# All k and q of slots 6 to 23 transposed by DMA, with token tiles of 4,2,2,2,2,4,4,4 slots

## The chip, the cores and the metric

The kernel runs on one core of a Trainium2 chip. The metric is device time in microseconds (us), from the start of one execution to its end. The core has five engines that run side by side, each with its own queue in order: TensorE (PE in the profile; PEld is its weight loads), VectorE (DVE), ScalarE (ACT), GpSimd (POOL) and SyncE (SP), which here only issues DMAs. Matrix products land in PSUM banks, from which ACT or DVE must carry them to on-chip memory (evict them). Sixteen DMA engines move data between on-chip memory and HBM, and can transpose on the way.

## The reference

Two stages. The first is a recurrent linear attention (retention) over 4 sequences of 768 tokens with 8 heads of 64. The second is a bilinear feed-forward layer over the 3072 tokens that result.

```python
gamma = 1.0 - 2.0 ** (-5.0 - np.arange(H))          # one decay for each head
scale = 1.0 / np.sqrt(D)
for t in range(S):
    state = gamma[None, :, None, None] * state + np.einsum('bhd,bhe->bhde', k[:, :, t], v[:, :, t])
    y[:, :, t] = scale * np.einsum('bhd,bhde->bhe', q[:, :, t], state)
x = y.transpose(0, 2, 1, 3).reshape(B * S, H * D)    # 3072 x 512
a = x @ w_a                                          # 512 -> 1536
b = x @ w_b
return (a * b) @ w_out                               # 1536 -> 512
```

Inputs and output are float32; the kernel multiplies in bfloat16 and accumulates in float32.

## The kernel before

**Slots.** The 3072 tokens are cut into 24 slots of 128 tokens, six for each sequence. Slots 0 to 5 are done in pairs by functions of their own (names that end in 2). For slots 6 to 23, `load_slot` (line 84) fetches k, q and v of a slot, 256 KB each, through SP. `casts` (line 221) scales k and q by tables of powers of gamma, which turns the decay into a plain causal product, and converts them and v to bfloat16, all on POOL.

**Transposes.** The attention needs k and q with the head dimension on the partitions (`kqT`). For slots from `ON_PE` = 10 on, `casts` issues one DMA transpose on SP (line 228), and behind it the loads of the slot two further on. For slots 6 to 9, `flip` (line 234) does it on PE with eight transposes into a PSUM bank, and DVE copies the bank out. The loads of slots 6 to 11 stand in the list `LOADS` at the start.

**Turns.** Slots go through the attention two at a time. `turn(new, old)` (line 316) begins two slots and ends the two before. For the new ones it adds k and v products into the state (`update`, whose result is cast to `gst` by the engine given, ACT unless DVE is named), and multiplies k by q (`scores`: the second slot into two banks of the pool `ff`, the first into one of its own; DVE masks both into `aT`). For the old ones it adds the part from the state (`inter`) and the part within the slot (`intra`) into `y`, which ACT copies to `xt` (`leave`). The state is begun anew with each sequence: slots 6, 12 and 18 have no `inter`, and slots 11, 17 and 23 no `update`.

**Token tiles.** The feed-forward layer works on tiles of several slots, listed in `TILES`: 4, 2, 4, 4, 4, 4, 2. For each of twelve blocks of 128 hidden columns, `ffn_ab` makes `a` (four matmuls, evicted by ACT to `asb`) and `g` (four matmuls, multiplied with `asb` by DVE into `ht`). A tile of 4 slots has 512 columns for each matmul, one of 2 slots 256. `ffn_out` makes one slot's output from `ht` with twelve matmuls; ACT evicts it to `osb`. For tiles 0 and 1 the store is held back and issued by SP at the next piece of feed-forward work; from tile 2 on ACT issues it at once (lines 483 to 486). `a`, `g`, output products, flips and the second slot's scores share the three banks of `ff`.

**What sets the order.** Every instruction is chained to the one before it on its engine (`seq`), so each engine works in the order of the program text. From tile 1 on, `run` (line 488) goes through a tile's blocks and outputs and puts turns and flips in at the places given (lines 575 to 586); it calls `casts` for a slot four pieces of work ahead of its flip. The transposed tiles have six buffers, the scaled ones six, the raw loads three pairs, `osb` four. A buffer is written again only once its last reader is done.

Of the kernel before, what the change touches and what calls it, by code (L numbers as in the profile page):

```python
# [10 lines left out]
BF16 = mybir.dt.bfloat16  # L11
# [1 line left out]
ALU = mybir.AluOpType  # L13


TILES = [4, 2, 4, 4, 4, 4, 2]
PAIRS = 3
ON_PE = 10


LOADS = "p0 p1 w0 w1 w2 w3 w4 p2 w5 o0 o1 o2 o3 o4 o5 s6 s7 s8 s9 s10 s11".split()


@with_exitstack
def kernel(
# [10 lines left out]
    nc = tc.nc  # L36
    P = 128
    B, H, S, D = q.shape
    NCH = S // P
    HP = H // 2  # L40
# [3 lines left out]
    NFT = DFF // P  # L44
    NSLOT = B * NCH
# [14 lines left out]
    tra = ctx.enter_context(tc.tile_pool(name="tra", bufs=4))  # L60
# [4 lines left out]
    psff = ctx.enter_context(tc.tile_pool(name="psff", bufs=3, space=bass.MemoryType.PSUM))  # L65
# [7 lines left out]
    def seq(bi):  # L73
        ins = bi.ins
        prev = last.get(ins.engine)
        if prev is not None:
            tc.add_manual_dep(ins, prev.name, nosync, reason="program order")
        last[ins.engine] = ins
        return bi
# [4 lines left out]
    def load_slot(t):  # L84
        b, ci = divmod(t, NCH)
        for nm, src in (("k", k), ("q", q), ("v", v)):
            if t % 2 == 0:
                whole[nm] = raw.tile([P, 2, H, D], F32, tag=nm + "f", name=nm + "f")
            raws[nm, t] = whole[nm][:, t % 2]
            s = src[b, :, ci * P : (ci + 1) * P, :].rearrange("h p d -> p h d")  # L90
            seq(nc.sync.dma_start(out=raws[nm, t], in_=s))
# [21 lines left out]

    pending = list(LOADS)

# [6 lines left out]
    kqb = {}  # L122
    kqb = {}
# [8 lines left out]
    ident = const.tile([P, P], BF16, name="ident")  # L132
# [45 lines left out]
    def cast(engine, dst, src):  # L178
        if engine is nc.scalar:
            seq(nc.scalar.copy(dst, src))  # L180
        else:
            seq(engine.tensor_copy(dst, src))  # L182
# [10 lines left out]
    kb, qb, vb, kqT, aT = {}, {}, {}, {}, {}  # L193
    state = {}
    xt, where = {}, {}
    first = 0
    for J, n in enumerate(TILES):
        for i in range(n):
# [17 lines left out]
    def new_nat(t):  # L216
        kqb[t] = nat.tile([P, 2, HP, 2, D], BF16, tag="kqb", name="kqb")
        kb[t], qb[t] = kqb[t][:, 0], kqb[t][:, 1]
        vb[t] = nat.tile([P, H, D], BF16, tag="vb", name="vb")

    def casts(t):
        new_nat(t)
        scaled(nc.gpsimd, t, 0)
        scaled(nc.gpsimd, t, 1)
        cast(nc.gpsimd, vb[t], raws["v", t])
        if t >= ON_PE:
            kqT[t] = tra.tile([P, 2, HP, P], BF16, tag="kqT", name="kqT", bufs=6)
            seq(nc.sync.dma_start_transpose(
                out=kqT[t].rearrange("p a b c -> p (a b) c"),
                in_=kqb[t].rearrange("p a hp r d -> p (a hp r d)")))  # L230
            if t + 2 < NSLOT:
                load_slot(t + 2)

    def flip(t):
        if t >= ON_PE:
            return
        tp = psff.tile([P, 2, HP, P], BF16, tag="ff", name="tp")
        for hp in range(HP):
            seq(nc.tensor.transpose(tp[:, 0, hp, :], kb[t][:, hp, :, :], ident))  # L239
        for hp in range(HP):  # L240
            seq(nc.tensor.transpose(tp[:, 1, hp, :], qb[t][:, hp, :, :], ident))  # L241
        kqT[t] = tra.tile([P, 2, HP, P], BF16, tag="kqT", name="kqT", bufs=6)
        seq(nc.vector.tensor_copy(kqT[t], tp))

    def half(i):
        return slice(64 * i, 64 * i + 64)
# [17 lines left out]
    def update(t, eng):  # L264
        ci = t % NCH
        if ci == NCH - 1:
            return
        if ci == 0:
            state[0] = psst.tile([P, HP, D], F32, tag="st", name="st")
        st = state[0]  # L270
        for hp in range(HP):
            for r in range(2):
                seq(nc.tensor.matmul(st[half(r), hp, :], kb[t][:, hp, r, :],  # L273
                                     vb[t][:, HP * r + hp, :],
                                     start=(ci == 0 and hp == 0), stop=(hp == HP - 1),
                                     skip_group_check=True))
        cast(eng, gst[(t + 1) % 4], st)
# [38 lines left out]
    def turn(new, old, eng=nc.scalar):  # L316
        if old is not None:
            ys[old // 2] = [psat.tile([P, 4, P], F32, tag=f"y{r}", name="y") for r in range(2)]
        if new is not None:
            update(new, eng)  # L320
            scores(new + 1, True)
            scores(new, False)
        if old is not None:
            inter(old)
            inter(old + 1)
        if new is not None:
            update(new + 1, nc.scalar)
        if old is not None:
            intra(old)
            intra(old + 1)  # L330
            leave(old)
# [102 lines left out]
    def ffn_a(J, ft, c0=0, c1=None):  # L434
        c1 = TILES[J] * P if c1 is None else c1
        if J not in ht:
# [9 lines left out]
    def ffn_g(J, ft, c0=0, c1=None):  # L446
        c1 = TILES[J] * P if c1 is None else c1
        fs = slice(ft * P, (ft + 1) * P)
        g = psff.tile([P, 4 * P], F32, tag="ff", name="g")[:, : c1 - c0]
        for kt in range(KT):  # L450
            seq(nc.tensor.matmul(g, wb_bf[:, kt, fs], xcols(J, kt, c0, c1),  # L451
                                 start=(kt == 0), stop=(kt == KT - 1)))
        seq(nc.vector.tensor_tensor(ht[J][:, ft, c0:c1], g, asbs.pop((J, ft, c0)), op=ALU.mult))  # L453

    def ffn_ab(J, ft):
        store()
        ffn_a(J, ft)
        ffn_g(J, ft)
# [8 lines left out]
    def ffn_out(J, i):  # L467
        store()
        n0 = (sum(TILES[:J]) + i) * P
        osb = osbp.tile([P, DM], F32, tag="osb", name="osb")  # L470
        ends = J == len(TILES) - 1 and i == TILES[J] - 1
        cols = [(0, DM // 2), (DM // 2, 3 * DM // 4), (3 * DM // 4, DM)] if ends else [(0, DM)]
        for c0, c1 in cols:
            o = psff.tile([P, DM], F32, tag="ff", name="o")[:, : c1 - c0]
            for ft in range(NFT):
                seq(nc.tensor.matmul(o, ht[J][:, ft, i * P : (i + 1) * P], wo_bf[:, ft, c0:c1],  # L476
                                     start=(ft == 0), stop=(ft == NFT - 1)))
            cast(nc.vector if c0 == DM // 2 else nc.scalar, osb[:, c0:c1], o)
            if c0 == DM // 2:
                continue  # L480
            b0 = DM // 2 if c0 else 0
            dst, src = out[n0 : n0 + P, b0:c1], osb[:, b0:c1]
            if J < 2:
                held.append((dst, src))
            else:
                seq((nc.sync if c0 else nc.scalar).dma_start(out=dst, in_=src))

    def run(work, todo, ahead=4):
        order = []
        for g, w in enumerate(work):  # L490
            order += [what for at, *what in todo if at == g]
            order.append(w)
        starts = [a[0] for fn, *a in order if fn is flip]
        for i, (fn, *args) in enumerate(order):
            for fn2, *a2 in order[i : i + ahead + 1]:
                if fn2 is flip and a2[0] in starts:
                    starts.remove(a2[0])
                    casts(a2[0])
            fn(*args)

    D_, G_, A_ = nc.vector, nc.gpsimd, nc.scalar
    K, Q = 0, 1
    warm(11, psat, "y1")
# [64 lines left out]
    ffn_g(0, 11)  # L568
    for j in range(NO):
        cast_o(j)  # L570
    work = [(ffn_ab, 1, ft) for ft in range(NFT)]
    work += [(ffn_out, 0, i) for i in range(TILES[0])]
    work += [(ffn_out, 1, i) for i in range(TILES[1])]
    V_ = nc.vector
    run(work, [(11, flip, 6), (13, flip, 7), (14, turn, 6, None, V_), (14, flip, 8), (15, flip, 9),
               (16, flip, 10), (16, turn, 8, 6, V_), (17, turn, None, 8), (17, flip, 11)])
    todo = {2: [(4, turn, 10, None), (4, flip, 12), (6, flip, 13), (9, turn, 12, 10), (9, flip, 14),
                (10, flip, 15), (13, flip, 16), (14, flip, 17), (14, turn, 14, 12, V_)],
            3: [(4, turn, 16, 14), (4, flip, 18), (6, flip, 19), (9, turn, 18, 16),
                (10, flip, 20), (12, flip, 21)],  # L580
            4: [(4, turn, 20, 18), (4, flip, 22), (6, flip, 23), (9, turn, 22, 20)],
            5: [(4, turn, None, 22)],
            6: []}
    for J in range(2, len(TILES)):
        run([(ffn_ab, J, ft) for ft in range(NFT)] + [(ffn_out, J, i) for i in range(TILES[J])],
            todo[J])


# [28 lines left out]
```

## Time and profile before

| | us |
|---|---|
| median of three runs | 234.96 (233.38 to 236.01) |
| profiled execution | 235.0 |
| its span, first to last instruction | 233.3 |
| PE busy | 224.9 (96%) |
| DVE busy | 95.7 (41%) |
| ACT busy | 83.8 (36%) |
| POOL busy | 78.0 (33%) |
| mean granted TensorE clock | 0.993 |

A row of the page's second part cuts the span into 40 slices of 5.83 us and gives the busy share of each in tenths. The chain that ended last follows the work back from the last instruction, at each step to what released it. A line of a timeline gives the start, the length, the engine, the line of the code, the operation with its tiles, and the count; in brackets stands the idle time before it and what ended that. Matmuls are pipelined, so their recorded lengths overlap; the time from start to start tells what one holds PE for. SPq and ACTq are the DMA issues of SP and ACT.

### The profile page before, as it was taken

The numbers are of one execution on the slowest core, as the hardware profiler recorded it, in microseconds if no ns is written. First come the engines' busy times: TensorE is split into PE (matmuls) and PEld (weight loads), VectorE is DVE, ScalarE is ACT, GpSimd is POOL, SyncE is SP. The second block draws the span as 40 slices with busy tenths as digits, with TensorE's granted clock in tenths as the row PEclk, the third lists the DMA queues.
The fourth block names the chain that finished last, engine by engine and source line by source line (L and its number), as shares of the span: only waits on it lengthen the run. The fifth ranks groups of instructions, "written<-read, shape, count | busy, mean of one in ns | idle before, by whom it ended". The sixth has DMA issues, their size and how long they took to land.

```text
span 233.3 us, 5013 instructions
## 1 busy us (share of the span) xinstructions
PE 224.9 (96%) x2047; PEld 122.4 (52%) x2068; DVE 95.7 (41%) x171; ACT 83.8 (36%) x163; POOL 78.0 (33%) x98
## 2 busy tenths in 40 slices
PE   7879999999999999999999999999999999999995
PEld 2556545587555444545454544454544444445874
DVE  3783338744444264624164630164720233310530
ACT  3362434342215333524344522353422343322422
POOL 4355667787674416454444440000000000000000
PEclk9997999999999999999999999999999999999999
DMA  6999999999999999999999983200002200012102
GB/s 174 290 332 349 343 270 362 368 219 220 198 234 252 273 201 214 173 236 234 250 225 168 240 131 104 90 4 0 3 0 93 90 0 0 0 48 90 45 3 90
DMA packets 91894, 38.59 MB, mean 165 GB/s; under 512 B 71776, under 2 KB 87392, under 8 KB 91872
## 3 DMA queue, kind: packets, MB, share of 16 engines
q1 hardware_dynamic: 89280, 33.69, 64.5%
q10 hardware_dynamic: 2592, 4.59, 5.7%
q8 instruction: 16, 0.26, 0.5%
q14 instruction: 6, 0.05, 0.1%
HBM read 28.31 MB, written 6.29 MB: 148 GB/s over the span
## 4 chain that ended last, share of the span: by engine, by line
PE 80%; DMA 11%; SPq 5%; POOL 1%; issue 1%; ACT 1%; ACTq 0%
PE o L476 27%; PE a L441 23%; PE g L451 23%; DMA wstb<-in_moe_w_b_dram 11%; SPq L97 3%; PE at L257 2%; PE y L302 2%; SPq L105 2%; PE st L273 2%; POOL wb_bf L182 1%; PE y L293 1%; PE tp L239 0%; PE y L406 0%; PE tp L241 0%; ACT osb L180 0%
## 5 line engine op out<-in xcount | busy, mean ns | idle before, releaser
L453 DVE TENSOR_TENSOR ht<-g,asb 128x512 bf16<-128x512 f32 (+1 forms) x86 | 52.0, 604 | 108.0 <-PE g L451 83.1
L441 PE MATMUL a<-xt,wa_bf 128*128 128x512 bf16 (+1 forms) x337 | 76.3, 346 | 1.5 <-POOL wa_bf L182 1.0
L451 PE MATMUL g<-xt,wb_bf 128*128 128x512 bf16 (+1 forms) x341 | 76.3, 347 | 0.4 <-ACT asb L444 0.2
L444 ACT CAST asb<-a 128x512 bf16<-128x512 f32 (+1 forms) x86 | 44.3, 517 | 69.8 <-PE a L441 66.9
L476 PE MATMUL o<-wo_bf,ht 128*128 128x512 bf16 (+2 forms) x303 | 63.7, 362 | 0.5
L451 PEld LDWEIGHTS <-wb_bf 128*128 128x128 bf16 x344 | 33.9, 99 | 29.1 <-issue 0.6
L441 PEld LDWEIGHTS <-wa_bf 128*128 128x128 bf16 x344 | 32.9, 98 | 28.7 <-POOL wa_bf L182 1.2
L476 PEld LDWEIGHTS <-ht 128*128 128x128 bf16 x312 | 29.2, 98 | 31.4
L214 POOL TENSOR_TENSOR kqb<-kf,ktab 128x512 bf16<-128x512 f32 x22 | 22.9, 1043 | 37.0 <-DMA kf<-in_k_dram 36.6
L180 ACT COPY osb<-o 128x512 f32<-128x512 f32 (+2 forms) x25 | 14.1, 565 | 53.5 <-PE o L476 38.0
L262 DVE TENSOR_TENSOR aT<-at,mask 128x512 bf16<-128x512 f32 x36 | 22.3, 680 | 0.0
L182 POOL CAST vb<-vf 128x512 bf16<-128x512 f32 x24 | 15.4, 648 | 12.6 <-DMA vf<-in_v_dram 12.3
L214 POOL TENSOR_TENSOR kqb<-qf,qtab 128x512 bf16<-128x512 f32 x18 | 18.8, 1042 | 1.3 <-DMA qf<-in_q_dram 0.8
L311 ACT CAST xt<-y 128x512 bf16<-128x512 f32 x18 | 9.7, 589 | 3.0 <-PE y L302 3.0
L427 PE MATMUL idle<-zero 128*128 128x512 bf16 x22 | 7.6, 473 | 1.3 <-DVE zero L126 1.3
L370 DVE TENSOR_TENSOR aT<-at,mask 128x512 bf16<-128x512 f32 x12 | 7.4, 681 | 1.1 <-PE at L364 1.1
L182 POOL CAST wb_bf<-wstb 128x1024 bf16<-128x1024 f32 x6 | 6.3, 1042 | 4.1 <-DMA wstb<-in_moe_w_b_dram 4.1
L182 POOL CAST wa_bf<-wsta 128x1024 bf16<-128x1024 f32 x6 | 6.3, 1042 | 2.3 <-DMA wsta<-in_moe_w_a_dram 2.2
L182 POOL CAST wo_bf<-wsto 128x1024 bf16<-128x1024 f32 x6 | 6.3, 1042 | 2.1 <-DMA wsto<-in_moe_w_out_dram 2.1
L180 ACT CAST gst<-st 128x256 bf16<-128x256 f32 x12 | 4.5, 372 | 6.7 <-PE st L273 6.7
L257 PE MATMUL at<-kqT 64*64 64x128 bf16 x288 | 5.8, 219 | 0.0
L302 PE MATMUL y<-aT,vb 128*64 128x128 bf16 x144 | 5.6, 221 | 0.0
(50 smaller groups left out, 83.6 us busy)
## 6 DMA issues: line engine op xcount, KB each, us to landing
kf<-in_k_dram SPq DMA_DIRECT2D x18, 256.0 KB, 4.7
qf<-in_q_dram SPq DMA_DIRECT2D x18, 256.0 KB, 4.9
vf<-in_v_dram SPq DMA_DIRECT2D x18, 256.0 KB, 5.1
out_dram<-osb ACTq DMA_DIRECT2D x17, 256.0 KB, 2.0
wsta<-in_moe_w_a_dram SPq DMA_DIRECT2D x6, 512.0 KB, 8.8
wstb<-in_moe_w_b_dram SPq DMA_DIRECT2D x6, 512.0 KB, 8.9
wsto<-in_moe_w_out_dram SPq DMA_DIRECT2D x6, 512.0 KB, 8.8
kf<-in_k_dram SPq DMA_DIRECT2D x3, 512.0 KB, 7.1
```

Source lines behind the costliest of these rows:

```text
L180: seq(nc.scalar.copy(dst, src))
L182: seq(engine.tensor_copy(dst, src))
L214: seq(eng.tensor_tensor(dst, src, tab, op=ALU.mult))
L257: seq(nc.tensor.matmul(at[r][half(c), hp, :], kqT[t][half(r), 0, hp, half(c)], kqT[t][half(r), 1, hp, :], start=True, stop=True, skip_grou ...
L262: seq(nc.vector.tensor_tensor(aT[t][:, r], at[r], mask.to_broadcast([P, HP, P]), op=ALU.mult))
L302: seq(nc.tensor.matmul(ys[t // 2][r][half(c), 2 * (t % 2) + j, :], vb[t][:, HP * r + hp, :], aT[t][:, r, hp, :], start=begin(t, c, r), sto ...
L311: seq(nc.scalar.copy(xt[J][:, 2 * r : 2 * r + 2, i * P : (i + 2) * P].rearrange("p j (s n) -> p j s n", s=2), ys[t // 2][r].rearrange("p ( ...
L441: seq(nc.tensor.matmul(a, wa_bf[:, kt, fs], xcols(J, kt, c0, c1), start=(kt == 0), stop=(kt == KT - 1)))
L444: seq(nc.scalar.copy(asb, a))
L451: seq(nc.tensor.matmul(g, wb_bf[:, kt, fs], xcols(J, kt, c0, c1), start=(kt == 0), stop=(kt == KT - 1)))
L453: seq(nc.vector.tensor_tensor(ht[J][:, ft, c0:c1], g, asbs.pop((J, ft, c0)), op=ALU.mult))
L476: seq(nc.tensor.matmul(o, ht[J][:, ft, i * P : (i + 1) * P], wo_bf[:, ft, c0:c1], start=(ft == 0), stop=(ft == NFT - 1)))
```

## The change

The PE path for transposes goes, and slots 6 to 9 are transposed by DMA like the others. The loads of slots 8 to 11 leave the list at the start; each is now issued by `casts` behind a transpose. The tiles become 4, 2, 2, 2, 2, 4, 4, 4. In `turn`, where the second new slot has no update (it is a sequence's last), the update of the first moves behind `inter`. The order from tile 1 on, which `run` made, is written out: turns are followed by one, two or three output products of an earlier tile, or by blocks.

```diff
-TILES = [4, 2, 4, 4, 4, 4, 2]
+TILES = [4, 2, 2, 2, 2, 4, 4, 4]
 PAIRS = 3
-ON_PE = 10
-LOADS = "p0 p1 w0 w1 w2 w3 w4 p2 w5 o0 o1 o2 o3 o4 o5 s6 s7 s8 s9 s10 s11".split()
+LOADS = "p0 p1 w0 w1 w2 w3 w4 p2 w5 o0 o1 o2 o3 o4 o5 s6 s7".split()
...
         cast(nc.gpsimd, vb[t], raws["v", t])
-        if t >= ON_PE:
-            kqT[t] = tra.tile([P, 2, HP, P], BF16, tag="kqT", name="kqT", bufs=6)
-            seq(nc.sync.dma_start_transpose(
...
-            if t + 2 < NSLOT:
-                load_slot(t + 2)
-
-    def flip(t):
...
+        seq(nc.sync.dma_start_transpose(
+            out=kqT[t].rearrange("p a b c -> p (a b) c"),
+            in_=kqb[t].rearrange("p a hp r d -> p (a hp r d)")))
+        if t + 2 < NSLOT:
+            load_slot(t + 2)
...
     def turn(new, old, eng=nc.scalar):
...
+        two = new is not None and (new + 1) % NCH < NCH - 1
         if new is not None:
-            update(new, eng)
+            if two or old is None:
+                update(new, eng)
             scores(new + 1, True)
             scores(new, False)
...
-        if new is not None:
+        if two:
             update(new + 1, nc.scalar)
+        elif new is not None and old is not None:
+            update(new, eng)
...
+    casts(6)
+    blocks(1, 0, 3)
+    casts(7)
+    blocks(1, 3, NFT)
+    casts(8)
+    outs(0, 0, 1)
+    casts(9)
+    turn(6, None, V_)
+    outs(0, 2, 3)
+    casts(10)
+    turn(None, 6)
+    outs(1, 0)
+    casts(11)
+    blocks(2, 0, 6)
+    casts(12)
+    turn(8, None, V_)
+    outs(1, 1)
+    casts(13)
+    blocks(2, 6, NFT)
+    turn(10, 8)
+    casts(14)
+    outs(2, 0)
+    blocks(3, 0, 6)
+    casts(15)
+    outs(2, 1)
+    blocks(3, 6, NFT)
+    turn(12, 10, V_)
+    casts(16)
+    outs(3, 0)
+    blocks(4, 0, 3)
+    casts(17)
+    blocks(4, 3, 6)
+    turn(14, 12, V_)
+    casts(18)
+    outs(3, 1)
+    blocks(4, 6, NFT)
+    casts(19)
+    turn(16, 14, V_)
+    casts(20)
+    outs(4, 0, 1)
+    blocks(5, 0, 3)
+    casts(21)
+    blocks(5, 3, 6)
+    turn(18, 16)
+    casts(22)
+    blocks(5, 6, 8)
+    casts(23)
+    blocks(5, 8, NFT)
+    outs(5, 0)
+    turn(20, 18)
+    outs(5, 1, 2, 3)
+    blocks(6, 0, 4)
+    turn(22, 20)
+    blocks(6, 4, 9)
+    turn(None, 22)
+    blocks(6, 9, NFT)
+    outs(6, 0, 1, 2, 3)
+    blocks(7, 0, NFT)
+    outs(7, 0, 1, 2, 3)
```

`blocks(J, a, b)` calls `ffn_ab` for blocks a to b - 1 of tile J, and `outs(J, ...)` calls `ffn_out` for the slots named.

More of the change, by code (lines that the diff above doesn't have):

```diff
@@ L225, in casts @@
         cast(nc.gpsimd, vb[t], raws["v", t])
-        if t >= ON_PE:
-            kqT[t] = tra.tile([P, 2, HP, P], BF16, tag="kqT", name="kqT", bufs=6)
-            seq(nc.sync.dma_start_transpose(
-                out=kqT[t].rearrange("p a b c -> p (a b) c"),
-                in_=kqb[t].rearrange("p a hp r d -> p (a hp r d)")))
-            if t + 2 < NSLOT:
-                load_slot(t + 2)
-    def flip(t):
[L235 to L241, printed above, removed]
-        kqT[t] = tra.tile([P, 2, HP, P], BF16, tag="kqT", name="kqT", bufs=6)
-        seq(nc.vector.tensor_copy(kqT[t], tp))
+        kqT[t] = tra.tile([P, 2, HP, P], BF16, tag="kqT", name="kqT", bufs=6)
+        seq(nc.sync.dma_start_transpose(
[3 more added lines that the diff above has]
+            load_slot(t + 2)
     def half(i):
@@ L486, in ffn_out @@
                 seq((nc.sync if c0 else nc.scalar).dma_start(out=dst, in_=src))
[L488 to L499, printed above, removed]
     D_, G_, A_ = nc.vector, nc.gpsimd, nc.scalar
@@ L570, with blocks, outs @@
         cast_o(j)
-    work = [(ffn_ab, 1, ft) for ft in range(NFT)]
-    work += [(ffn_out, 0, i) for i in range(TILES[0])]
-    work += [(ffn_out, 1, i) for i in range(TILES[1])]
     V_ = nc.vector
[L575 to L586, printed above, removed]
+    def blocks(J, a, b):
+        for ft in range(a, b):
+            ffn_ab(J, ft)
+    def outs(J, *rows):
+        for i in rows:
+            ffn_out(J, i)
+    casts(6)
[57 more added lines that the diff above has]
+    outs(7, 0, 1, 2, 3)
 _INS = ['q', 'k', 'v', 'moe_w_a', 'moe_w_b', 'moe_w_out']
```

## The prediction

> **What bounds the kernel now.** I read the page's 40 slices first, then the chain that ended last, then TensorE's (PE's) timeline around each part that the change touches, then ScalarE's (ACT's) and the load queue's (SP's).
>
> ```profile
> PE   7879999999999999999999999999999999999995
> ...
> PEclk9997999999999999999999999999999999999999
> DMA  6999999999999999999999983200002200012102
> ...
> PE o L476 27%; PE a L441 23%; PE g L451 23%; DMA wstb<-in_moe_w_b_dram 11%; SPq L97 3%; PE at L257 2%; PE y L302 2%; SPq L105 2%; PE st L273 2%; POOL wb_bf L182 1%; PE y L293 1%; PE tp L239 0%; PE y L406 0%; PE tp L241 0%; ACT osb L180 0%
> ```
>
> PE is full from slice 8 (about 45 us) to the end, at a granted clock of 9 tenths or more, and the chain runs through it; before that it runs through weight loads. The DMA engines are full too, until slice 22 (about 135 us). The change begins with `casts(6)`, so the first 45 us stay. Behind them the end moves by what PE's own work loses or gains, plus any wait that reaches PE. Starts in PE's timeline show that work closely packed, so I price by start to start:
>
> ```profile
> 54.54 0.60 PE L451 MATMUL g<-xt,wb_bf 128*128 128x256 bf16 x4
> 54.98 0.39 PE L239 MATMUL tp<-ident,kqb 128*128 128x128 bf16 x4
> 55.20 0.39 PE L241 MATMUL tp<-ident,kqb 128*128 128x128 bf16 x4
> 55.42 0.60 PE L441 MATMUL a<-xt,wa_bf 128*128 128x256 bf16 x4
> ```
>
> A flip (eight transposes) moves the next matmul by 0.44 us. All of this is one execution of 235.0 us (span 233.3, 1.7 around it); the median of the runs is 234.96, so a change against one is a change against the other.
>
> **The change, part by part.**
>
> *Four flips go.* 54.98 to 55.42, 58.96 to 59.40, 63.17 to 63.63, 66.22 to 66.66: 0.44 + 0.44 + 0.46 + 0.44 = **-1.78 us**, all on PE. Their four VectorE (DVE) copies (0.69 us each) go as well; DVE is 41% busy and PE waited for none of them: 0.
>
> *One tile of four slots becomes two of two.* The list goes from five tiles of 4 and two of 2 to four and four. An a/g pair of 512 columns takes 1.725 us start to start (195.16 to 202.06 is four pairs), one of 256 columns 0.873 (46.68 to 54.54 is nine). Twelve blocks times (2 x 0.873 - 1.725) = **+0.25**. Its cover is that weight loads (98 ns each) fit under 109 ns a matmul: 9.05 us of weight loads stood in the 10.19 us of tile 1. The output products stay 24.
>
> *What follows an output product.* ACT evicts it, issues its store, and only then evicts the next block's `a`; three `ff` banks let PE get only `a`, `g`, `a` ahead. For 512 columns that covers it. Where 256 columns follow, before has one such place:
>
> ```profile
> 214.15 0.60 PE L441 MATMUL a<-xt,wa_bf 128*128 128x256 bf16 x4
> 214.35 0.59 ACT L180 COPY osb<-o 128x512 f32<-128x512 f32 x1 [2.00 <-PE o L476]
> ...
> 214.96 0.34 ACTq L486 DMA_DIRECT2D out_dram<-osb  x1
> 215.02 0.60 PE L441 MATMUL a<-xt,wa_bf 128*128 128x256 bf16 x4
> ...
> 215.40 0.65 ACT L444 CAST asb<-a 128x256 bf16<-128x256 f32 x2 [0.47 <-PE g L451]
> ...
> 215.82 0.60 PE L451 MATMUL g<-xt,wb_bf 128*128 128x256 bf16 x4 [0.20 <-ACT asb L444]
> ```
>
> The second `g` should start at 215.46 and starts at 215.82: 0.36 us. After the change this place is gone (-0.36; last tile has 4 slots), and there are four: products (2,0), (2,1), (3,0), (3,1), each followed by blocks of two-slot tiles and stored from ACT (lines 483 to 486: tiles from 2 on). 4 x 0.36 - 0.36 = **+1.08**. Products of tiles 0 and 1 are stored from SP, so ACT saves the 0.34 and `g` is just met: 0.
>
> *Turns.* Their number stays 11. In before (8,6) took 1.72 (69.25 to 70.97), (none,8) and (10,none) 1.02 each. In their place come (none,6) 1.02, (8,none) and (10,8), which like (16,14) has one update: 1.70. (8,none) casts `gst` on DVE, and now follows a 256-column block whose 0.42 us `ht` is ahead: cast from about 0.69 to 1.11 us into the turn, where `update(9)` wants to start at 0.81: 1.02 + 0.33. Together 4.07 against 3.76: **+0.3**.
>
> *Turn (20,18)* now comes right behind product (5,0) with its `gst` cast on ACT. By the fence above ACT is free 1.25 us behind the product; cast 0.37; `update(21)` could begin at about 1.7 and would be due at 1.02 (before's turn (14,12), also behind a product, casts on DVE: 105.93 to 106.95). **+0.65**. In (10,8) and (16,14) the moved update only shifts work: 0.
>
> *Load queue.* Four transposes are added to a full queue. SP issues in order; transposes 6 to 9 now stand ahead of the loads of slots 8 to 11, and store (0,0) ahead of transpose 9, (0,1) and (0,2) ahead of 10, (0,3) ahead of 11, (1,0) ahead of 12. If PE waits for none, the cost is 0; the cover is lateness that is still allowed. In before one transpose and three loads cycle in 4.4 to 6.3 us without a store between:
>
> ```profile
> 85.17 1.92 SPq L228 DMA_TRANSPOSE kqT<-kqb  x1
> 87.14 0.58 SPq L91 DMA_DIRECT2D kf<-in_k_dram  x1
> 87.77 0.63 SPq L91 DMA_DIRECT2D qf<-in_q_dram  x1
> 88.44 0.97 SPq L91 DMA_DIRECT2D vf<-in_v_dram  x1
> 89.58 2.01 SPq L228 DMA_TRANSPOSE kqT<-kqb  x1
> ```
>
> I take 4.8, the mean of the four cycles from 85.17 to 104.41, and 0.7 per store (its share at that rate of loading). Transpose 6 waits for GpSimd's q of slot 6 (50.61); transpose 7 is issued at 55.5 and lands 4.6 later (3.0 to 6.3 is what landing takes): 60.1. PE needs it for `scores(7)`: 45.23 + 12 x 0.873 + two products of 2.59 + 0.35 into the turn = 61.3. Transpose 11: 55.5 + 4 x 4.8 + 4 x 0.7 = 77.5, lands 82.1; turn (10,8) wants it at 85.4 by the terms above. From turn (12,10) on (about 103) the spare time grows. So I take 0, with bounds 0 and, at 5.7 a cycle and 6.3 to land, +3: nothing lets a full queue gain.
>
> **Sum:** -1.78 + 0.25 + 1.08 + 0.3 + 0.65 = **+0.5 us**: 235.0 becomes 235.5.
>
> **The Trainium skill, weighed.** A flip's eight transposes show 220 ns each as records, but 55 ns each start to start. The Trainium skill, "TensorE: Matmul & The Clock Gate", Part 4: PE-mode transpose, gives about 275 ns for one in a kernel's context. By it 32 would cost 8.8 us, and the sum would be 228.5; the fence of the flip speaks against it, as the next `a` starts 0.44 us behind the first transpose.
>
> **Rivals.**
>
> 1. *ACT's stalls don't come* (the 0.36 at 215 being peculiar to four products in a row, and the update's wait swallowed): without 1.44 and 0.65 it is 233.4. For it: single products leave ACT idle before them. Against: in the fence ACT also idled 2.00 us before that product. Chance 0.2.
>
> 2. *The load queue is late, slower than before.* Place: `scores(7)` and `scores(11)`. For: the queue has no idle slice, and cycles of 5.7 and 6.3 occur. From a mean cycle of about 5.5 both deadlines are passed; at 5.7 with 6.3 to land the waits add to 2 to 3 us, and 238 results. Against: at 4.8 there are 1.2 and 3.3 us to spare. Chance 0.16.
>
> 3. *ACT is held by its stores.* Each transfer takes one of eight semaphores in turn, and its issue waits until the transfer that had it has landed. Before once shows this:
>
> ```profile
> 113.04 0.59 ACT L180 COPY osb<-o 128x512 f32<-128x512 f32 x1 [2.00 <-PE o L476]
> 114.47 0.34 ACTq L486 DMA_DIRECT2D out_dram<-osb  x1
> 114.85 0.59 ACT L444 CAST asb<-a 128x512 bf16<-128x512 f32 x1 [1.22 <-PE g L451]
> ```
>
> The store could go at 113.63 and goes at 114.47: 0.84 late; 512-column blocks hid all but 0.06. If all four singly dealt stores meet a full queue like this, 256-column blocks hide nothing: 235.5 + 4 x 0.84 = 238.9. Against: three other stores of that tile went at once. Chance 0.1.
>
> 4. *Transposes cost PE what their records say* (32 x 220 ns = 7.0 us): 235.5 + 1.78 - 7.0 = 230.3. Start times speak against it: 0.02.
>
> That the change doesn't do what it says I rule out: without the flip lines no PE transpose is left from slot 6 on.
>
> **Numbers.** Forecast (235.0 to 236.2) 0.45; rivals 0.2, 0.16, 0.1, 0.02; 0.07 for what I don't see, on both sides. About 1% (2.35 us) is what a measurement can tell from no change here; the three runs of before spread by 2.6. Slower by over 1%: most of rivals 2 and 3 and some unseen, 0.25; faster by over 1%: rival 4, unseen, and rival 1 with a low draw, 0.09; within: 0.66. The range takes in rival 1's 233.4 and rival 2's 238: 233.2 to 238.2; it leaves out rival 3 at its full price.
>
> **What would show it.** No transposes on PE behind 45 us, and 18 transposes on SP. `g` of blocks (3,1), (3,7), (4,1), (4,7) late by 0.3 to 0.4, released by ACT's `asb`. In turn (20,18) the second `st` waits for `gst` by ACT. No wait of `at` for a DMA at about 61 and 85 us; one of over a microsecond there proves rival 2. ACT gaps over 0.3 us between an `osb` cast and its store are rival 3. Wrong altogether I would be if the first 45 us moved, or if the clock fell in the two-slot tiles (before: 1.00 in tile 1).

## The result and the profile after

The changed kernel takes a median of **237.39 us** (235.64 to 239.04, 22 runs) against 235.70 (233.38 to 240.18, 22 runs) for the kernel before. The ratio is **1.0085 [1.0057, 1.0112]**: slower by 0.85%, some 2.0 us. (It leaves out runs over 1.5% above the fastest of their kernel; the medians above are of all runs and lie 1.7 us apart.) The forecast was +0.5 us, the same within 1%, with a range of 233.2 to 238.2. The sign, the class and the range hold; the price is four times too small, and 237.39 lies outside the band of 235.0 to 236.2 that the forecast gave a chance of 0.45.

The profiled execution took 236.9 us, its span 235.2. From its page, the rows that answer to those of before: PE's and DMA's busy tenths, the granted clock, and the chain that ended last, by engine and by line.

```profile
PE   7979999999699998999999999989999999999994
PEclk9999999999999999999999999999999999999999
DMA  6999999999999999999999996201200002200022
PE 65%; DMA 22%; SPq 6%; ACT 2%; POOL 2%; issue 1%; ACTq 1%; DVE 0%; POOLq 0%; DVEq 0%
PE o L467 20%; PE g L442 20%; PE a L432 19%; DMA kf<-in_k_dram 8%; DMA wstb<-in_moe_w_b_dram 8%; SPq L96 3%; DMA wsta<-in_moe_w_a_dram 3%; DMA kqT<-kqb 3%; PE at L244 2%; SPq L104 1%; PE y L289 1%; ACT osb L179 1%; POOL kqb L213 1%; PE st L260 1%; SPq L226 1%
```

Slice 10 (58.8 to 64.7 us) shows PE at 6 tenths, where before it was full. The chain now leaves PE in the middle: DMA holds 22% of it where it held 11%, and `kqT<-kqb` (a DMA transpose) and `kf` (the loads ahead of it) have come in. DMA stays at 9 tenths for one slice more than before, through slice 23.

PE's timeline of the changed kernel shows the places; in brackets the idle time and what ended it.

```profile
59.62 0.32 PE L260 MATMUL st<-vb,kqb 128*64 128x64 bf16 x8
61.84 0.64 PE L244 MATMUL at<-kqT 64*64 64x128 bf16 x32 [1.90 <-DMA kqT<-kqb]
...
92.64 0.60 PE L442 MATMUL g<-xt,wb_bf 128*128 128x256 bf16 x4 [1.04 <-ACT asb L435]
...
100.84 0.60 PE L442 MATMUL g<-xt,wb_bf 128*128 128x256 bf16 x4 [0.20 <-ACT asb L435]
...
158.54 0.32 PE L260 MATMUL st<-vb,kqb 128*64 128x64 bf16 x8 [0.62 <-ACT gst L179]
```

The first pair is `scores(7)` in turn (none,6): PE has the state products done and waits 1.90 us for the transpose of slot 7. At 92.64 `g` of block (3,1), behind product (2,0), is held 1.04 by ACT. The row at 158.54 is `update(21)` in turn (20,18).

The load queue on SP, and below it the traffic between 54 and 62 us in slices of 0.2 us, show why slot 7 is late:

```profile
55.37 2.40 SPq L226 DMA_TRANSPOSE kqT<-kqb  x1
```

```profile
GB/s 288 210 115 84 134 241 252 262 287 287 291 287 247 227 220 227 223 216 202 188 292 200 113 36 13 0 8 10 9 10 257 289 305 273 288 270 227 209 220 220
```

The transpose is issued at 55.37 (foreseen: 55.5) and lands just ahead of the wait's end, at 61.80 by the trace (foreseen: 60.1), 6.4 us later. The transfers ahead of it fill the queue until 58.5, and then for 1.4 us, 58.6 to 60.0, almost nothing moves at all (at most 36 GB/s, where 220 to 290 are usual).

ACT's timeline at product (2,0):

```profile
90.33 0.59 ACT L179 COPY osb<-o 128x512 f32<-128x512 f32 x1 [1.73 <-PE o L467]
91.75 0.38 ACTq L477 DMA_DIRECT2D out_dram<-osb  x1
92.22 0.65 ACT L435 CAST asb<-a 128x256 bf16<-128x256 f32 x2 [1.31 <-DMA kf<-in_k_dram]
```

The eviction ends at 90.92; the store could go then and goes at 91.75, and the row of the next cast names as releaser the landing of a load of k. The trace's own records of the DMA issues, which these views don't print, give the semaphore of each transfer: eight numbers in all, dealt out in turn over the issues of SP and ACT. This store has number 110. The load of k that was issued at 86.61 had it before, and landed at 91.67, 0.08 us ahead of the store. That is rival 3's mechanism: the store waits for the transfer that last had its semaphore, and PE's next `g` waits behind the store and the cast.

### The profile page after: what moved, and what is told of

Read it like the earlier page. It is cut to its first block, busy times and chain, and to the rows that moved or that the text cites. A ratio compares the mean times of both kernels' runs of the same rounds, so it can differ in the third digit from the quotient of the medians.

```text
span 235.2 us, 5207 instructions
## 1 busy us (share of the span) xinstructions
PE 223.7 (95%) x2132; PEld 129.0 (55%) x2132; DVE 95.6 (41%) x181; ACT 84.4 (36%) x173; POOL 77.1 (33%) x98
## 4 chain that ended last, share of the span: by engine, by line
PE 65%; DMA 22%; SPq 6%; ACT 2%; POOL 2%; issue 1%; ACTq 1%; DVE 0%; POOLq 0%; DVEq 0%
PE o L467 20%; PE g L442 20%; PE a L432 19%; DMA kf<-in_k_dram 8%; DMA wstb<-in_moe_w_b_dram 8%; SPq L96 3%; DMA wsta<-in_moe_w_a_dram 3%; DMA kqT<-kqb 3%; PE at L244 2%; SPq L104 1%; PE y L289 1%; ACT osb L179 1%; POOL kqb L213 1%; PE st L260 1%; SPq L226 1%
## 5 line engine op out<-in xcount | busy, mean ns | idle before, releaser
L444 DVE TENSOR_TENSOR ht<-g,asb 128x256 bf16<-128x256 f32 (+1 forms) x98 | 53.9, 550 | 108.4 <-PE g L442 79.8
L432 PE MATMUL a<-xt,wa_bf 128*128 128x256 bf16 (+1 forms) x392 | 78.5, 323 | 1.5 <-POOL wa_bf L181 1.5
L442 PE MATMUL g<-xt,wb_bf 128*128 128x256 bf16 (+1 forms) x392 | 78.1, 322 | 1.6 <-ACT asb L435 1.4
L435 ACT CAST asb<-a 128x256 bf16<-128x256 f32 (+1 forms) x98 | 46.0, 473 | 70.1 <-PE a L432 67.5
L442 PEld LDWEIGHTS <-wb_bf 128*128 128x128 bf16 x392 | 38.2, 98 | 25.9 <-issue 2.3
L432 PEld LDWEIGHTS <-wa_bf 128*128 128x128 bf16 x392 | 37.7, 98 | 26.2 <-POOL wa_bf L181 1.7
L181 POOL CAST vb<-vf 128x512 bf16<-128x512 f32 x24 | 14.5, 610 | 17.0 <-DMA vf<-in_v_dram 14.3
L418 PE MATMUL idle<-zero 128*128 128x512 bf16 x24 | 8.4, 491 | 1.3 <-DVE zero L125 1.3
L179 ACT CAST gst<-st 128x256 bf16<-128x256 f32 x10 | 3.7, 373 | 11.2 <-PE st L260 10.8
L244 PEld LDWEIGHTS <-kqT 64*64 64x64 bf16 x288 | 4.5, 106 | 3.1 <-DMA kqT<-kqb 2.0
```

The costliest lines, as they stand in the source:

```text
L244: seq(nc.tensor.matmul(at[r][half(c), hp, :], kqT[t][half(r), 0, hp, half(c)], kqT[t][half(r), 1, hp, :], start=True, stop=True, skip_grou ...
L418: seq(nc.tensor.matmul(idle, zero[:, 0, :], zero, start=True, stop=True, skip_group_check=True))
L432: seq(nc.tensor.matmul(a, wa_bf[:, kt, fs], xcols(J, kt, c0, c1), start=(kt == 0), stop=(kt == KT - 1)))
L435: seq(nc.scalar.copy(asb, a))
```

## The experiments

To compare executions I use one measure beside the time: the **stretch** from the first 256-column `a` of tile 1 (45.23 in before's profile, 43.73 in after's) to the start of the last matmul (230.17 and 231.80). It leaves out the start phase, which the change doesn't touch. It is 184.94 us in the profile of before that the prediction was made from, and 188.07 in after's: +3.13. That is the prediction's +0.5, plus 1.90 at `scores(7)`, plus about 0.7 from the held store (1.04 instead of 0.36). A stretch is of one execution, and the start of tile 1 differs between executions by up to 1.8 us (43.49 to 45.30); where that matters it is said.

The theory: the change's work on PE and ACT costs what the prediction's terms say, and the rest is lateness of the load queue, which four more transposes make longer; it reaches PE at `scores(7)` and through ACT's stores. Rivals: the new order costs more than the terms say; or the waits are single faults, each of which could be mended by itself.

**V behind the next transpose.** Each load of v from slot 8 on is issued one transpose later, so that a transpose has fewer loads ahead of it.

```diff
-    def load_slot(t):
+    def load_slot(t, names="kqv"):
...
         for nm, src in (("k", k), ("q", q), ("v", v)):
+            if nm not in names:
+                continue
...
+        if 8 <= t + 1 < NSLOT:
+            load_slot(t + 1, "v")
         if t + 2 < NSLOT:
-            load_slot(t + 2)
+            load_slot(t + 2, "kq")
```

> The changed kernel with one edit: each slot's v is loaded behind the next slot's transpose, so transpose 7 has two loads ahead of it and not three. Theory 'the load queue is late': in the profile of the changed kernel the scores of slot 7 waited 1.90 us for transpose 7; it should land one transfer, about 1.2 us, earlier, the wait should be 0 to 0.7 us, and the time 1.2 to 1.9 us below the changed kernel's, some 0.1 to 0.8 us above before. Rival 'the transpose itself is slow' (6.4 us from its issue to its landing): the wait stays at 1.5 us or more and the time stays 2.0 us above before.

Measured: 240.80 us (238.20 to 242.23), ratio 1.0151 [1.0085, 1.0218], no faster than the change itself. PE's timeline of this kernel:

```profile
61.19 0.32 PE L264 MATMUL st<-vb,kqb 128*64 128x64 bf16 x8
61.43 0.64 PE L248 MATMUL at<-kqT 64*64 64x128 bf16 x32
...
92.41 0.60 PE L446 MATMUL g<-xt,wb_bf 128*128 128x256 bf16 x4 [1.10 <-ACT asb L439]
...
101.98 0.60 PE L446 MATMUL g<-xt,wb_bf 128*128 128x256 bf16 x4 [1.58 <-ACT asb L439]
```

The wait at `scores(7)` is gone: 61.43 follows 61.19 with nothing between. The transpose landed at 58.2, in time for a tile 1 that starts early or late. This execution started it late, at 45.30, and without the edit would have waited some 0.4 there, not 1.90: the profile of the next experiment, which starts tile 1 at 45.24 with after's queue, waits 0.41, and its `scores(7)` start at 61.86 as after's do at 61.84. But the `g` behind product (2,1), 0.20 late in after, is 1.58 late here: its eviction ended at 99.72, its store went at 101.13, released by a load of v. The stretch is 187.63, against 188.07 in after, and the time isn't lower. A wait has come up at the next place; mending this one place gains nothing.

**The stores of tiles 2 and 3 on SP.**

```diff
-            if J < 2:
+            if J < 4:
                 held.append((dst, src))
```

> The changed kernel with the outputs of tiles 2 and 3 stored from SP, as those of tiles 0 and 1 are. Theory 'ACT is held by its stores': the second g behind products (2,0), (2,1), (3,0), (3,1), late by 1.20, 0.37, 0.30 and 0.33 us in the changed kernel, comes on time; 2.2 us less, or 0.2 us below before. Rival 'the eviction of the product alone holds ACT': each stays late by some 0.3 us, and only the 0.84 us by which one store waited for a load goes: 1.2 us above before. The wait at the scores of slot 7 stays in both.

Measured: 239.23 us (237.72 to 242.26), ratio 1.011 [1.0053, 1.0167], above what either the theory or its rival expected. The four single products (2,0), (2,1), (3,0) and (3,1) no longer hold their `g`. The stores of tile 4, still ACT's, do. Timeline of this kernel, ACT and PE:

```profile
127.11 0.58 ACT L179 COPY osb<-o 128x512 f32<-128x512 f32 x1 [1.73 <-PE o L467]
130.91 0.38 ACTq L477 DMA_DIRECT2D out_dram<-osb  x1
131.38 0.58 ACT L179 COPY osb<-o 128x512 f32<-128x512 f32 x1 [3.69 <-PE g L442]
135.41 0.34 ACTq L477 DMA_DIRECT2D out_dram<-osb  x1
...
136.48 1.87 PE L442 MATMUL g<-xt,wb_bf 128*128 128x512 bf16 x4 [3.44 <-ACT asb L435]
```

Two stores are held 3.2 and 3.5 us (127.69 to 130.91, 131.96 to 135.41). PE loses 0.63 and 3.44 to them, and behind that the page shows the granted clock at 7 tenths in two slices (132 to 144 us): the 512-column `g` at 136.48 has a record of 1.87 instead of 1.02. Stores put into a full queue make everything behind them later, and the first stores left on ACT meet that: by the semaphore records the first of the two waited for a store that had been moved to SP (issued at 125.53, landed at 130.83), the second for a load of q (landed at 135.33).

**Turn (20,18) casts on DVE.**

```diff
-    turn(20, 18)
+    turn(20, 18, V_)
```

> The changed kernel with the gst cast of turn (20,18) on DVE in place of ACT. Theory: the 0.62 us for which the second update of that turn waited goes, and the time is 0.6 us below the changed kernel's, 1.4 us above before. Rival: DVE, which has four maskings of 0.68 us in that turn, casts no sooner, or the wait moves to the maskings' readers: no change, 2.0 us above before.

Measured: 237.96 us (236.15 to 239.51), ratio 1.0075 [1.0041, 1.0109]. The wait of `update(21)`, 0.62 in after, is gone, so this term was as predicted in place and size (0.65). The time doesn't show it: in this profile `scores(7)` waited 1.93 and four `g` waited 1.05, 0.20, 1.44 and 0.97, the last two where after had 0.17 and none. 0.6 us is less than the queue's waits differ between executions.

**DMA transposes alone.** The order and tiles of before; only the transposes of slots 6 to 9, and with them the loads of 8 to 11, go to the queue.

```diff
-ON_PE = 10
+ON_PE = 6
...
-LOADS = "p0 p1 w0 w1 w2 w3 w4 p2 w5 o0 o1 o2 o3 o4 o5 s6 s7 s8 s9 s10 s11".split()
+LOADS = "p0 p1 w0 w1 w2 w3 w4 p2 w5 o0 o1 o2 o3 o4 o5 s6 s7".split()
```

> The kernel before with one part of the change alone: slots 6 to 9 transposed by DMA, loads of slots 8 to 11 behind the transposes; tiles, order and turns as before. By the prediction's terms: 1.78 us of flips go. Theory 'the load queue is late': the scores of slot 7, due at about 61.2 us, wait for transpose 7 by 0.6 to 1.9 us, and the sum is 1.2 us below before to 0.1 above. Rival 'the queue is not late in itself' (the wait in the changed kernel came from a hole in the DMA traffic of that one execution): no wait, 1.8 us below before.

Measured: 240.12 us (237.23 to 241.60), ratio 1.0137 [1.0076, 1.0198]: some 3.2 us slower, against an expectation of a small gain. PE's timeline of this kernel:

```profile
62.05 0.64 PE L257 MATMUL at<-kqT 64*64 64x128 bf16 x32 [1.78 <-DMA kqT<-kqb]
...
71.23 0.64 PE L257 MATMUL at<-kqT 64*64 64x128 bf16 x32 [1.08 <-DMA kqT<-kqb]
...
83.61 1.44 PE L441 MATMUL a<-xt,wa_bf 128*128 128x512 bf16 x4 [2.90 <-ACT osb L180]
```

`scores(7)` and `scores(9)` wait for their transposes. The third wait is a new kind: ACT stood 3.92 us before an `osb` eviction because an earlier output's store, on the late SP queue, had not yet emptied the buffer. The page shows the clock at 8 and 7 tenths in two slices around these waits (60 to 66 and 84 to 90 us); in the trace's records it is at half from 63.60 to 67.02 and from 84.08 to 87.50. The stretch is 192.45, 9.3 above what the terms say without the flips. The three waits are 5.8 of it, and half of 2 x 3.4 us is another 3.4, by my estimate. So the transposes by themselves cost more than the flips, and the new order of the change, which puts output products between turns, takes part of that back.

**The order alone.** The tiles and order of after, with the flips of 6 to 9 on PE and the loads of 8 to 11 at the start.

```diff
-LOADS = "p0 p1 w0 w1 w2 w3 w4 p2 w5 o0 o1 o2 o3 o4 o5 s6 s7".split()
+LOADS = "p0 p1 w0 w1 w2 w3 w4 p2 w5 o0 o1 o2 o3 o4 o5 s6 s7 s8 s9 s10 s11".split()
...
+        if t >= 10:
...
+    def flip(t):
...
-    outs(0, 0, 1)
+    flip(6)
+    outs(0, 0)
+    flip(7)
+    outs(0, 1)
...
-    blocks(2, 0, 6)
+    blocks(2, 0, 2)
+    flip(8)
+    blocks(2, 2, 4)
+    flip(9)
+    blocks(2, 4, 6)
```

> The changed kernel with slots 6 to 9 transposed on PE as before (four flips between the pieces of work, loads of slots 8 to 11 in the list at the start): tiles, order and turns of the change alone. By the prediction's terms without the flips' gain: 0.25 + 1.08 + 0.3 + 0.65, or 2.3 us above before. Theory 'the load queue is late because of the four transposes': no wait at the scores of slot 7, and no store of tiles 2 and 3 held on ACT by over 0.3 us, so that 2.3 us it is. Rival 'the order itself puts the stores in a bad place': stores still held, and with the flips added 3 us or more above before.

Measured: 236.13 us (235.47 to 237.38), ratio 1.0022 [0.9988, 1.0055], not to be told from before. No wait for a transpose is left in PE's timeline. The stretch is 187.13, +2.19 against the prediction's profile; the terms without the flips' gain say 0.25 + 1.08 + 0.3 + 0.65 = +2.28. The rival that the new order costs more than its terms falls. What it leaves open is why a kernel whose work is 2.2 us longer takes the same time as before; the repeats of before, below, answer that.

**Fewer loads.** After's kernel, but v of slots 8 to 13 is not loaded; their casts read v of slots 6 and 7 again. Six loads of 256 KB leave the queue. The attention of those slots is computed from v of 6 and 7, with as many instructions.

```diff
         for nm, src in (("k", k), ("q", q), ("v", v)):
+            if nm == "v" and 8 <= t < 14:
+                raws[nm, t] = raws[nm, 6 + t % 2]
+                continue
```

> The changed kernel without the loads of v for slots 8 to 13 (their casts read the v of slots 6 and 7, so six of 54 transfers are left out and the output is another): the queue is lighter by about 1.2 us per slot. Theory 'the load queue is late': the wait at the scores of slot 7 falls from 1.9 us to under 0.7, stores on ACT go at once, and what is left is the sum of the prediction, 0.5 us above before. Rival 'transposes are slow by themselves, stores wait for other reasons': 2.0 us above before, as the changed kernel.

Measured: 235.22 us (233.83 to 235.69), ratio 0.9965 [0.993, 1.0]: not 0.5 us above before, as the theory had it, but level with it or up to 0.7% below. Before has queue waits of its own, as its repeats will show, and the expectation didn't count them. PE's timeline of this kernel:

```profile
61.14 0.32 PE L263 MATMUL st<-vb,kqb 128*64 128x64 bf16 x8
61.38 0.64 PE L247 MATMUL at<-kqT 64*64 64x128 bf16 x32
...
91.58 0.60 PE L445 MATMUL g<-xt,wb_bf 128*128 128x256 bf16 x4 [0.32 <-ACT asb L438]
```

With a lighter queue the transpose of slot 7 is in time, the stores go at once, and the `g` behind product (2,0) is 0.32 late, close to the 0.36 that the prediction gave each of the four boundaries. The stretch is 185.48: **+0.54 where the terms sum to +0.5**. Nothing of the change is undone in this run, only the queue is shorter. But its profile (span 234.0) is of a late start, tile 1 at 45.25, which comes from a drop of the clock in the start phase (last section). The seven executions without that drop have spans of 232.1 to 234.0 us, median 233.2, where this stretch with a start 1.5 us earlier would give 232.5. So some of them may still wait, by up to 1.5 us. The next run, which starts early, leaves no such doubt.

**Fewer loads and no ACT holds.** The same, with `J < 4` for the stores on SP and `turn(20, 18, V_)`.

```diff
+            if nm == "v" and 8 <= t < 14:
+                raws[nm, t] = raws[nm, 6 + t % 2]
+                continue
...
-            if J < 2:
+            if J < 4:
...
-    turn(20, 18)
+    turn(20, 18, V_)
```

> The kernel with fewer loads (v of slots 8 to 13 left out), and in it the outputs of tiles 2 and 3 stored from SP and the gst cast of turn (20,18) on DVE. Theory: with a queue that is on time, the terms of the prediction come off one by one: the four late g (0.36 us each) and the late update (0.65) go, 2.1 us below the kernel with fewer loads, 1.6 us below before. Rival 'ACT's eviction of the product alone makes g late': the four g stay 0.2 us late or more, 0.8 us below before or above.

Measured: 232.13 us (231.96 to 233.84), ratio 0.9849 [0.9798, 0.9899]. PE's row of `scores(7)`, with no idle time before it:

```profile
59.69 0.64 PE L247 MATMUL at<-kqT 64*64 64x128 bf16 x32
```

The stretch is 183.33, -1.61; the terms without the four boundaries and turn (20,18) leave 0.5 - 1.44 - 0.65 = -1.6. Tile 1 starts at 43.55 here, as early as in after, and PE waits for no transfer and no store. (Against the runs of before beside it, median 235.82, the time is 3.7 us lower and not 1.6, as before has waits too.) With queue and ACT both out of the way the flips' 1.78 us is really gained. It is in the change, and the waits spend it.

**Two slots on PE.** After, with flips for slots 6 and 7, loads of 8 and 9 at the start, and the DVE cast in turn (20,18).

```diff
-LOADS = "p0 p1 w0 w1 w2 w3 w4 p2 w5 o0 o1 o2 o3 o4 o5 s6 s7".split()
+LOADS = "p0 p1 w0 w1 w2 w3 w4 p2 w5 o0 o1 o2 o3 o4 o5 s6 s7 s8 s9".split()
...
+        if t < 8:
+            return
...
-    outs(0, 0, 1)
+    flip(6)
+    outs(0, 0)
+    flip(7)
+    outs(0, 1)
...
-    turn(20, 18)
+    turn(20, 18, V_)
```

> The changed kernel with slots 6 and 7 transposed on PE (two flips of 0.44 us; loads of slots 8 and 9 in the list at the start), 8 and 9 by DMA, and the gst cast of turn (20,18) on DVE. Theory 'the load queue is late': 0.9 us of flips buy off the 1.9 us wait and make the queue lighter by two transposes, and 0.6 us come from the cast: 2.0 + 0.9 - 1.9 - 0.6, 0.4 us above before, less if the stores are no longer held. Rival 'the wait only moves on': PE comes sooner to the held stores, which grow by what the wait loses: 1.5 to 2 us above before.

Measured: 237.00 us (236.29 to 239.05), ratio 1.0057 [1.0022, 1.0092]. PE's timeline:

```profile
92.50 0.60 PE L453 MATMUL g<-xt,wb_bf 128*128 128x256 bf16 x4 [2.06 <-ACT asb L446]
...
101.58 0.60 PE L453 MATMUL g<-xt,wb_bf 128*128 128x256 bf16 x4 [1.10 <-ACT asb L446]
```

`scores(7)` waits for nothing (its first product starts at 60.65). The holds behind products (2,0) and (2,1), 1.04 and 0.20 in after, are 2.06 and 1.10: 1.92 more, where a wait of 1.90 went. (That the two are so alike is chance, since the flips take 0.88 of PE between them.) ACT's eviction of product (2,0) comes 1.17 us sooner than in after (89.16 against 90.33), and its store goes at almost the same time (91.59 against 91.75). A PE that comes sooner to a queue that doesn't waits at the next place.

**Before, twice again.** The kernel unchanged, for the waits of other executions than the one that the prediction read.

> The kernel before, unchanged, for another profile. In the profile that the prediction used, the clock was granted at half for 3.4 us in the start phase and tile 1 began at 45.2 us; in the changed kernel's it was not, and tile 1 began at 43.7. Theory 'the load queue, not PE, sets the pace of the next 60 us': in an execution without that drop tile 1 begins at about 43.6 us, PE then waits some 1.5 to 2.5 us for transfers that come no sooner, and from tile 1's first matmul to the last it is 186.5 to 187.5 us, against 184.94 in the first profile. Rival 'the drop simply costs 1.5 us': 184.9 again, and a span of 231.7.

> The kernel before once more, as the execution may or may not have the drop of the clock. With the drop, both theories expect 184.9 to 185.5 us from tile 1's first matmul to the last; without it, the queue theory expects 186.5 to 187.5 and the rival 184.9.

Measured: 236.38 and 235.84 us, the median of before beside them 235.98. Timeline of the second, PE's start of tile 1 and then ACT and PE behind product (2,3):

```profile
43.69 0.60 PE L441 MATMUL a<-xt,wa_bf 128*128 128x256 bf16 x4
...
111.50 0.58 ACT L180 COPY osb<-o 128x512 f32<-128x512 f32 x1 [2.00 <-PE o L476]
115.31 0.34 ACTq L486 DMA_DIRECT2D out_dram<-osb  x1
...
116.33 1.02 PE L451 MATMUL g<-xt,wb_bf 128*128 128x512 bf16 x4 [2.28 <-ACT asb L444]
```

The same product's store, held 0.84 us in the prediction's profile with 0.06 reaching PE, is held 3.23 here (112.08 to 115.31) and costs PE 2.28; in the first repeat 2.27. The stretches are 187.32 and 187.33, not 184.94. Tile 1 starts at 43.69 and 44.22, not 45.23: in both repeats the granted clock is 1.0 throughout, while the prediction's profile shows 7 tenths in slice 3. The hold is 2.39 us longer because ACT comes to it 1.54 sooner (111.50 against 113.04), and because the load of q whose semaphore the store takes lands 0.85 later (115.24 against 114.39). So before too has some 2.3 us of queue waits in these two, and the prediction had read an execution without them.

Neither repeat had the drop of the clock, so the other half of the theory, that the drop hides the wait, rests on the prediction's profile alone. The timed runs of before speak against it as a rule. Of 75 beside the experiments, 43 have a mean clock of 0.999 or more, and spans of 232.4 to 235.6 us, median 233.9; 32 have the drop (0.993 or less), with spans of 233.2 to 236.1, median 234.6. The last experiment gives the spans without the hold: 231.5 to 231.9, and 233.2 to 233.7 with the drop. None of the 43 comes down to that, and of the 32 only nine do. (The last experiment ran on one chip, the 75 on four.) So most executions of before are longer than one without the hold, with the drop or without it, and the prediction's was one of the few that aren't.

**The order without ACT's holds.** The order alone (above), with the stores of tiles 2 and 3 on SP and the DVE cast in turn (20,18).

```diff
-            if J < 2:
+            if J < 4:
...
-    turn(20, 18)
+    turn(20, 18, V_)
```

> The changed order and tiles with slots 6 to 9 transposed on PE, the outputs of tiles 2 and 3 stored from SP and the gst cast of turn (20,18) on DVE. The order alone measured 0.5 us above before. Theory: the four late g and the late update go, 2.1 us: 1.6 us below before, the fastest of the kernels that compute everything. Rival 'stores on SP come behind a late queue and hold ACT through the osb buffers', as in the kernel that moved those stores to SP with all transposes by DMA: no gain, 0.5 us above before or more.

Measured: 234.09 us (233.50 to 235.50), ratio **0.9919 [0.9889, 0.9949]**. The stretch is 185.06, +0.12; the terms say 2.28 - 1.44 - 0.65 = +0.19. From tile 1 to the last matmul no row of PE's timeline shows an idle time before it. Two differences to other stretches price single terms. Against the order alone it is 187.13 - 185.06 = 2.07 shorter, and the four late `g` and turn (20,18) were priced at 1.44 + 0.65 = 2.09. Against the fewer loads without ACT holds it is 185.06 - 183.33 = 1.73 longer, and of what differs only the four flips are PE's work: they were priced at 1.78.

**Before, with tile 2's stores on SP.** One character of the kernel before.

```diff
-            if J < 2:
+            if J < 3:
                 held.append((dst, src))
```

> The kernel before with the four outputs of tile 2 stored from SP in place of ACT, all else as before. In both new profiles of before the store of output (2,3) sat on ACT until the load that had its semaphore had landed, and PE idled 2.3 us. Theory 'the hold of that store is what before loses': it goes, and the time is 1.9 to 2.3 us below before. Rival 'a late queue only finds another place' (SP stores come late, osb buffers are not free): no gain, or a wait of ACT's osb cast for an output DMA.

Measured: 233.43 us (233.22 to 235.39), ratio **0.9936 [0.9907, 0.9966]**, with before beside it at 235.36. ACT's timeline at the same product:

```profile
111.58 0.58 ACT L180 COPY osb<-o 128x512 f32<-128x512 f32 x1 [2.01 <-PE o L476]
112.50 0.58 ACT L444 CAST asb<-a 128x512 bf16<-128x512 f32 x1 [0.33 <-PE a L441]
```

No store stands between the eviction and the next cast, and ACT waits only for PE. The stretch is 184.89, which is what the prediction's profile of before had, and from tile 1 on only the 0.20 at the boundary of tile 6 remains. This and the run above beat both kernels; between the two the intervals leave no order.

The stretches side by side, worked out from the start of tile 1 and of the last matmul in each trace; the terms are the prediction's for each kernel, with the waits for ACT in them (the late `g`, turn (20,18)) and with nothing for the queue:

| kernel | stretch | against 184.94 | terms |
|---|---|---|---|
| before, the prediction's profile | 184.94 | 0 | 0 |
| before, repeated | 187.32, 187.33 | +2.4 | 0 |
| after | 188.07 | +3.13 | +0.5 |
| V behind the next transpose | 187.63 | +2.7 | +0.5 |
| stores of tiles 2 and 3 on SP | 191.21 | +6.3 | -0.94 |
| turn (20,18) casts on DVE | 189.82 | +4.9 | -0.15 |
| DMA transposes alone | 192.45 | +7.5 | -1.78 |
| two slots on PE | 188.23 | +3.3 | +0.73 |
| order alone | 187.13 | +2.19 | +2.28 |
| after, fewer loads | 185.48 | +0.54 | +0.5 |
| the same, no ACT holds | 183.33 | -1.61 | -1.6 |
| order alone, no ACT holds | 185.06 | +0.12 | +0.19 |
| before, tile 2's stores on SP | 184.89 | -0.05 | 0 |

Where a row lies well above its terms, the rest is the waits told above. The stores on SP and the DMA transposes alone also lost some 2.5 and 3.4 us to the clock (an estimate: half of the time in which PE worked at half clock).

## Why the prediction was right, and where it failed

**What bounds it: right.** PE's own work carries the end from tile 1 on. Wherever the queue was kept out, the stretch moved by the sum of PE's starts, to 0.1 us.

**Flips, -1.78, and the tile split, +0.25: right within what the sums show.** The flips come out as the 1.73 between two runs without waits, which is also the end of rival 4 (7.0). The tile split was not measured singly; the sums that hold it came out at +0.54 for +0.5 and -1.61 for -1.6.

**`g` behind single products, 4 x 0.36: right as a floor.** With a light queue the three that show in the profile were 0.32, 0.20 and 0.16 idle. The idle time is less than the delay: at the prediction's own fence the profile gives 0.20 of idle time for a `g` that came 0.36 late. Together with turn (20,18) the four measured 2.07 for 2.09. Rival 1 (the stalls don't come) falls.

**Turns, +0.3, and turn (20,18), +0.65: right.** Turn (8,none) took 1.42 in after (76.59 to 78.01; foreseen 1.35), (10,8) 1.67 (85.86 to 87.53; foreseen 1.70), and `update(21)` waited 0.62.

**"Load queue. So I take 0, with bounds 0 and +3": this step failed.** In after's profile it measured 1.90 at `scores(7)` and about 0.7 through the store at 91.75, together 2.6: near the upper bound. Rivals 2 and 3 both came, each in part. The issue of transpose 7 was foreseen to 0.13 us. Its landing was not: I took 4.6 us from a stated 3.0 to 6.3, and it took 6.4, of which 1.4 was a hole in all traffic. The time at which PE needs it was wrong too: 61.3 was counted from a start of tile 1 at 45.23, and in after's profile it is 59.95, since tile 1 starts at 43.73. Landing 1.7 later and needed 1.35 earlier, against 1.2 of cover: that is the 1.90. The 1.2 us that I counted as cover were the delay of one execution's start. `scores(11)`, the second place of rival 2, was in time: transpose 11 landed at 83.94 for a need at 85.94.

**Rival 3 was dismissed on "three other stores of that tile went at once".** The one late store was the warning. In the two repeats of before the same store cost PE 2.27 and 2.28, through 512-column blocks that hid all but 0.06 in the profile I read.

**The yardstick.** "A change against one is a change against the other" also fails: the profile of before was one execution in which the queue's waits happened to be hidden. That they weigh on both kernels is why the time moved by 2.0 and not by 3.1, and that is luck: one wait that I priced at 0 in after (2.6) was for the most part made good by another that I had not seen in before (2.4). The range held because rival 2's 238 was taken into it, not because the sum was near. Between the two profiles of one clock (after 236.9, the second repeat 235.84) the stretch differs by 0.74 and the time by 1.1. The other 0.9 or so of the 2.0 I can't place by rows: after's runs spread over 3.4 us and its profile lies 0.5 below its median.

**What is shown and what isn't.** Shown: the change's own work is worth +0.5; a shorter queue takes the rest away; where one wait is removed, one at the next place comes up (v behind the transpose, two slots on PE, stores on SP). Shown by the trace's records, not tried apart: that ACT's stores wait for a semaphore. Each held store named here goes 0.07 to 0.08 us after the landing of the transfer that had its semaphore before (after 91.67 and 91.75, before repeated 115.24 and 115.31, stores on SP 130.83 and 130.91, 135.33 and 135.41). Not settled: what makes the holes in the traffic, and why some executions of before escape the wait.

## What to carry to other kernels

Work that moves from a full engine to a full queue is paid for at more places than the first one where it is late; follow the queue to every wait that hangs on it (the tile itself, stores that share its semaphores, the buffers that those stores empty), and try it with a few loads left out, which tells work from waiting (look whether any wait is left in that run). Before a transfer's spare time is counted as cover, look at it in several executions: here 1.2 us of spare time was the late start of a single one. And where an engine evicts for a full PE, let it issue no store while loads are in flight, unless what takes the stores instead has room: for the kernel before that was worth 0.6%, and in after's longer queue the same edit gained nothing.

## What the runs showed of the hardware

**A start that halves the clock for a while.** In some executions of most of these kernels the granted clock is at half for 3.4 us in the start phase (18.45 to 21.86 us in before's profile, whose slice 3 shows 7 tenths; mean clock 0.993 instead of 1.0). In kernels without queue waits this separates the spans: 231.5 to 231.9 against 233.2 to 233.7 us for before with tile 2's stores on SP, 230.0 to 230.4 against 231.9 for after with fewer loads and no ACT holds. In before the two groups overlap (medians 233.9 and 234.6): what PE gains by the undisturbed start it loses, in part, at the held store. The Trainium skill, "TensorE: Matmul & The Clock Gate", Part 1, gives the gate's window as 3413 ns, free-running, with half clock as the only other state it names for the gate itself; the 3.4 us at 0.5 in the trace agrees. Of the ramp at the start the Trainium skill says in the same part that it costs less than 1% of a typical kernel span and is not to be fitted to a count. The drop here is another thing, as the clock had been full from 4.8 us on; its 1.5 us are 0.6% of the span. But it moves PE against the queue: with after's queue, `scores(7)` waited 1.90 us without the drop and 0.41 with it (the profile with the stores on SP).

**Holes in full traffic.** The 1.4 us in after are not alone. The prediction's trace of before has, at 97.2 to 98.8 us, eight slices of 0.2 us with at most 45 GB/s; its second repeat has one of 1.4 us from 83.0 on, and after a second one of 1.2 us from 76.4 (at most 51 GB/s). Where one falls on a transfer that is needed, that transfer is late by as much.

**What a transpose takes of the queue.** From landing to landing in the full queue a 256 KB transpose took about 0.98 us and a 256 KB load 1.19, so four transposes lengthen it by some 3.9 us. The Trainium skill, "Advanced Engine Details and Errata", X-Bar Transpose (TRN2), says that transposes are as fast as regular DMAs, and expects 350 to 400 GB/s; the first agrees with these rows, the rate does not (256 KB in 0.98 us is 267 GB/s, in a queue shared with loads).
